# Re and im interleaved over partitions, half swaps with a stride of two and five swap buffers, in an adaLN + long convolution + MLP kernel whose order is laid out anew

## Chip, cores and metric

The kernel runs on one core of one Trainium2 chip. The metric is the device time of the program in microseconds (us), lower is better. The page of a profile has its own length, the span: the time from the first to the last instruction of one profiled execution.

## What is computed

One block of a conditioned network over x = A_q, with B = 1, S = 2048 positions, D = 640 channels and a hidden width F = 1728, in bf16:

```python
mod = (silu(c) @ w_mod).reshape(...)            # sa, ca, ga, sb, cb, gb
h = layernorm(x) * (1 + ca) + sa                # plays q
k_shift = sum_t k_pad[t:t+S] * shift_k[:, 3-t]  # causal, 4 taps
kv = k_shift * v
y = irfft(rfft(pad(kv, 4096)) * rfft(pad(ssm_k, 4096)))[:S] + kv * ssm_D
x = x + ga * (h * y)                            # part A
h = layernorm(x) * (1 + cb) + sb
u = gelu(layernorm(h) @ w1)
# four quarters of u, moved by +1, -1, +2, -2 positions -> hs
x1 = h + hs @ w2
x = x + gb * (x1 + gelu(layernorm(x1) @ w3) @ w4)   # part B
```

Part A is a convolution over the whole sequence, done with Fourier transforms of length 4096; part B is a two-stage MLP with a mixing of positions in its first stage.

## The kernel before

**Layout.** The positions stand on the 128 partitions in 16 tiles of 128, with 640 channels on the free axis; channels come in 5 blocks (ND). All SBUF regions are made once and reused many times: Ra (the filter, later x_all, that is x), Rb (inputs of the first stage, then products TAB, then y_all), T01 (its halves T0 and T1: data between the two transform stages, later weights w3 and w4), R3 (spectrum of kv, later the gelu results), R5 (k and v, then the spectrum of the filter, then h_all and scratch), RG (table Gs, then w1 and w2), RH (table Hs), RK, RQ. PSUM has four places.

**Stages.** Tables of sines come first: angles (L306 to L310), the Sin calls (`turns_to` L316, `sin_to` L321), the second-stage table Gs with its negated part (L348) and its copies to other partitions (L353, L354), the tables EA and EB of the inverse (L370). Then for both filter and kv: 32x32 transposes (`to_slots`, DVE, L394), first stage matmuls (L407) and second stage matmuls (`stage2_half`, L427), each followed by an evacuation of PSUM on ACT (L207) or DVE (L209). The result of a second stage has real parts on partitions 0 to 63 and imaginary parts on 64 to 127. The matmul of L463 makes k_shift. The modulation vectors are matmuls too (`mod_half`, L493, its weights loaded at L487). The layer norm of x (`ln1_stats`: DVE L539 and L540, or ACT L547 and L548; `ln1_fin` on POOL, L557 to L562) and the products that make q (`make_q`, L601 and L602, with the normalisation at L592 on ACT or L594 on DVE) are spread between these.

The complex product of the two spectra needs, beside a spectrum, the same spectrum with real and imaginary halves exchanged. `inverse1` does this ten times (5 blocks by 2 halves): two DMAs of 256 KB (L613, one issued by SP, one by POOL) exchange the halves into one of four buffers KSY, two DVE products follow (L617, the two in the tables TA and TB), then two groups of matmuls (L628 with EA, L629 with EB) and two evacuations. `inverse2` (matmul L661) makes y for up to three tiles in one PE task with two PSUM places. An identity matrix for PE's transposes is made on POOL (L644, shown as masks.py 197 and 199).

Part B runs over groups of tiles. `chain_a` multiplies y by q (L737), adds to x (L740) and squares on ACT (L729); `ln_finish` (POOL, L702 to L717) makes the statistics; `chain_b` applies the first norm (L751 or L756, and L755); `chain_c` the second (L724, or L592 and L594), and a `turn` transposes the tile by DMA (L765) or on PE (L772, evacuated at L778). `mm_w1` is L818 with gelu at L820, with an extra block of 32 rows (L828, gelu at L834); `mm_w2` L873 with its evacuation at L880; `mm_w3` L907 with gelu at L911; `mm_w4` L937 (and L928), the results added at L960 and L966 and stored at L969. Weights come by DMA: w1 and w2 at L992 to L995, w3 and w4 at L1009 to L1014. POOL fills up the last block of w3 (`L1020`). x is loaded in two parts (`x_load`, L525), the second with a dependence on the first tile of y (the list `y0`).

**What sets the order.** Every step is a task of a class Planner with the engine it may run on, its cost, and the regions it reads and writes. The order of all tasks, the engine of each and the PSUM place are not searched at run time, but written out in the string ORDER (L26 to L65); each word is a task's number, a letter for its engine (P, A, D, G for POOL, S for SP) and PSUM places. `Planner.run` (L120) emits the tasks in exactly this order:

```python
        for word in ORDER.split():
            head, _, places = word.partition(":")
            t = self.tasks[int(head[:-1])]
            t.on = self.CODE[head[-1]]
            assert t.deps <= seen and len(places) == len(t.alloc)
```

An engine runs its own tasks in that order and waits where data, a buffer or a PSUM place isn't there yet. In this order the 20 swaps run alternately on SP and POOL, of the 16 copies into Hs (L576) 7 are on SP and 9 on POOL, the identity comes after the last swap, and inverse2 of tiles 5 to 7 and 11 to 13 stand after the first w1 group.

Of the kernel before, what the change touches and what calls it, by code (L numbers as in the profile page):

```python
# [26 lines left out]
0S 2S 19G 18D 50G 20D 21G 23D 22D 25A 4S 3S 1S 6S 27G 29D 36G 37G 28D 5S 8S 9S 11S 68G 10S 69D 24A 26G 88P:0 72G 73D 31A 30A 32D 38G 66D 89A 84P:1 85A  # L27
67D 90P:2 91A 86P:3 87D 39G 40A 102P:0 103A 100P:1 76P:2 70G 104P:0 41D 49G 101A 77A 42G 43G 105A 106P:3 107A 44A 45G 33S 47S 46S 71D 34S 12S 35S 48S
184S 181S 183S 182S 13S 14S 116P:1 92P:2 98P:0 74D 75D 117D 7S 99A 118P:3 119D 114P:0 15S 112P:1 113D 93A 110P:2 16S 115A 111A 96P:3 97A 94P:0 95D
82P:2 83A 80P:1 81A 78P:3 108P:0 51D 109A 52D 54A 56G 57D 53A 122P:2 79D 155P:1 156A 153P:0 154A 151P:3 152A 123D 157P:2 136D 120P:1 121D 173P:0 158A  # L30
55G 174A 171P:3 172A 177P:2 178D 175P:1 176A 161P:0 162D 141P:3 142A 167P:2 168D 147P:1 148A 58G 59G 163P:0 164D 165P:3 166A 137P:2 138A 145P:1 146A
230D 17S 149P:0 150A 190D 188D 126P:3 127D 139P:2 140A 60A 143P:1 199S 144A 124P:0 125D 179P:2 180A 187D 169P:3 170A 234P:1 235A 244P:2 159P:0 160A
128P:3 231D 242P:1 243A 245A 130P:0 61G 62G 186D 63G 64A 238P:1 239A 129D 131D 232D 248P:2 65G 196S 249A 246P:3 247A 185D 189G 191A 252P:0 202S 253A
134P:1 135D 132P:2 133D 236P:3 240P:1 237A 260P:0 261A 233D 250P:2 251A 241D 423D 200P:3 201A 258P:0 259D 319G 208S 192G 268P:2 269A 318S 197P:3 205S
198A 266P:1 267A 272P:2 273D 270P:3 271A 203P:0 284P:1 285A 292P:2 211S 204D 278P:3 279A 417D 276P:0 277A 342S 293D 426D 209P:1 210D 294P:2 295D 226S
290P:3 222G 291A 280P:1 281D 229G 227S 264P:0 274P:2 275D 343G 223G 265A 256P:3 262P:1 420D 206P:0 207D 257A 225G 254P:2 255D 282P:3 263A 286P:0
288P:1 287D 224G 312P:2 220S 283A 289A 212P:3 321D 320D 218G 213D 313A 328D 304P:0 305A 308P:1 316P:2 317A 217S 216G 302P:0 219S 214G 418D 228S 298P:2
215S 324P:3 325D 309A 221G 327G 326S 329D 322P:1 303A 336D 306P:0 299A 421D 323A 310P:2 296P:3 307A 334S 335G 337D 350S 297A 311A 300P:1 330P:0 301A
351G 332P:3 344D 345D 331A 314P:2 333A 315A 359G 340P:1 341A 338P:0 352D 348P:3 349A 353D 346P:2 358S 347A 360D 361D 354P:1 367G 339A 356P:3 368D 366S
369D 355A 364P:2 357A 375G 362P:0 376D 372P:1 374S 377D 401S 193A 363A 382S 370P:3 373A 384D 383G 385D 380P:0 378P:1 365A 392D 390S 391G 393D 422D  # L40
419D 424D 402P:2 427D 194D 403D 371A 388P:3 381A 379A 407S 389A 428D 386P:0 387A 416G 425D 396P:1 397A 394P:3 395A 398S 399P:0 400D 432P:12 429A 430D
434D 433A 489D 502A 510D 195G 413S 490D 491A 511D 530D 408P:3 513D 404S 405P:0 406A 531D 409A 512A 440S 492G 494D 475P:12 476A 477A 515D 532A 462P:03
463A 410S 411P:1 493G 495D 514G 435S 533D 534G 496A 497D 498G 441G 535D 464A 516D 536D 518D 499D 412A 517A 469P:20 537A 471A 519G 500P:3 538D 539G
414P:1 465G 470A 558D 449S 501D 520D 521P:3 436S 415A 507P:0 522A 443S 559D 560A 540D 541P:2 437S 542A 466P:13 431D 561D 562D 563A 564D 508A 546P:2
467D 468A 547A 548P:1 565G 448S 570D 528P:0 571D 566D 572D 567D 549A 573A 446S 568D 505P:3 506A 569A 574G 575G 447S 509G 529A 503D 523D 504D 621D 622D
472P:21 473A 526P:3 527A 623A 579D 580P:0 581A 576D 439S 543A 524D 577P:2 525D 624D 578D 625D 444S 438S 550P:3 627D 480S 551D 481S 626A 590P:0 591A
445S 482S 552A 588P:2 589A 595P:3 459D 628G 633D 629D 634D 553G 630D 631D 632A 635D 637D 636A 479S 554G 555D 556P:0 557A 592P:2 486S 596D 597A 638G
641A 639D 478S 488G 610P:3 612P:0 611A 593D 608P:2 606P:3 544D 594A 598D 613A 599G 474D 460A 603D 600D 601P:1 604P:0 609A 457D 607A 442S 454A 602A
640S 642S 651P:2 649P:3 461G 650A 450D 487S 652A 485S 605D 673P:0 667P:1 451D 545D 668A 674A 452G 582D 583D 484S 689D 690D 456A 458G 584D 585D 656P:3
692D 693D 653P:2 483S 614P:1 654D 655A 657D 694A 615D 659G 658A 671P:0 695D 660G 664D 665P:2 691A 661D 662P:3 663D 453D 669P:1 696G 701A 702D 703D  # L50
666A 735P:3 455G 672A 670A 697D 698D 699D 705G 737P:2 736A 739P:0 733P:1 616D 704A 643D 644D 645D 700A 738A 706G 709A 675P:32 710S 586D 587D 740A 755D
756D 757A 646A 707D 708S 758D 759D 717P:0 714D 761G 760A 762G 734A 763A 767D 777A 768D 711A 769D 719P:1 764D 780D 676P 718A 720A 721P:0 724P:1 647D
712D 765D 766A 677D 678D 770A 680S 771G 772G 683D 741P:32 648D 773D 774S 722D 775A 776S 785P:0 725D 726A 783P:1 713D 723A 824D 617S 825D 742P 821D
822D 827D 679S 681S 826A 743D 682S 727G 728G 731D 732S 823A 784A 828G 829A 786A 787P:3 729D 730S 833D 834D 835D 830D 831D 832A 837D 684D 685S 836A
620S 838G 790P:1 788D 789A 839D 840S 799P:0 791D 805P:3 806A 781D 841D 715D 716D 881D 749D 793G 792A 882D 842S 883A 803P:1 804A 794G 795A 796S 845P:2
846A 797D 778D 779D 884D 843P:3 844A 885D 887D 800A 801P:1 802A 618S 847P:2 848D 782D 941D 850P:3 851D 852A 886A 849A 619S 687S 798S 865P:0 866A
859P:1 860A 863P:2 807P:30 861P:1 744D 750D 753S 942D 944D 745S 853D 854G 855A 888G 893A 943A 752S 857A 889D 864A 945G 890D 856S 808P 858S 809D 891D
946A 947D 948D 950D 894D 862A 892A 895D 896A 897G 925P:2 926A 898G 751S 815D 747S 919P:3 901D 686S 920A 923P:1 899D 921P:0 949A 951G 922A 902S 900S
905P:2 906A 688S 903P:3 904A 952D 953S 956P:0 957A 954P:2 955A 907P:3 908D 910P:0 810D 958G 748S 959P:2 911D 913G 746S 816D 819S 924A 962P:1 867P:30
960D 817S 963D 813S 754S 912A 993P:2 909A 914G 812S 868P 915D 916S 917D 918S 977P:1 978A 994D 995A 996G 997G 971P:2 820S 972A 869D 998A 875D 927P:30  # L60
818S 964A 814S 811S 876D 961A 965D 966G 973P:1 967A 999S 969A 970S 870D 929D 974A 1028P:2 930D 975P:3 928P 968S 1000P:1 1001A 931S 935D 1002P:0 934S
976A 979P:13 981D 1003A 1006P:0 871S 873S 1004P:1 879S 1005A 872S 874S 936D 980P 987D 1029A 937S 933S 1026P:1 939S 1007A 877S 932S 988D 1024P:2 1025A
1032D 880S 878S 982D 983S 1008P:30 986S 991S 1027A 989S 1033D 1010D 938S 940S 1022P:2 1011D 1023A 1014S 1013S 1009P 1016D 984S 985S 1017D 1030P:13
1034D 992S 990S 1015S 1012S 1018S 1019S 1020S 1035D 1037S 1036S 1021S 1038S 1031P 1040D 1039S 1041D 1043A 1045A 1042S 1044S
# [72 lines left out]
def kernel(  # L137
# [45 lines left out]
    Gs = RG[:, 0:6144].rearrange("p (k n) -> p k n", k=32)  # L183
# [8 lines left out]
    KSY = [(RG[:, 6144:8192], ("RG", 6144, 8192)), (RK[:, 0:2048], ("RK", 0, 2048)), (RK[:, 2048:4096], ("RK", 2048, 4096)), (Rb[:, 8192:10240], ("Rb", 8192, 10240))]  # L192
# [55 lines left out]
    offc = mem.tile([P, 6], F32, name="offc")  # L248

# [64 lines left out]
    def turns_to(dst, xs, n, r, w, neg=False):  # L314
        sc = (-2.0 if neg else 2.0) * PI_LO
        add("ACT", 0.23 + 0.00083 * n, lambda e: nc.scalar.activation(dst, xs, ACT.Sin, scale=sc), r=[r], w=[w])  # L316

    def sin_to(dst, ms, q, n, r, w, neg=False):
        b = (b_neg if neg else b_pos)[dst.start_partition():dst.start_partition() + dst.shape[0], :]
        sc = (2.0 if neg else -2.0) * PI_LO / q  # L320
        add("ACT", 0.25 + 0.00095 * n, lambda e: nc.scalar.activation(dst, ms, ACT.Sin, scale=sc, bias=b),  # L321
            r=[r, ("consts", 0, 1)], w=[w])
# [12 lines left out]
    for kb in range(2):  # L335
        o = (5120, 6656)[kb]
        k2s = slice(8 * kb, 8 * kb + 8)
        wk = ("RG", 1536 * kb, 1536 * kb + 1536, "g")
        pat, base = [[2, 8], [128, 64]], 1 + 16 * kb
        if kb == 0:  # L340
            ms, ma, ky = angles("R3", o, 512, pat, base, s64[:], 8192, (offc[:, 0:1], offc[:, 1:2]))
            ms3, ma3 = (t.rearrange("p (a b) -> p a b", a=8) for t in (ms, ma))
            sin_to(Gs[:, k2s, 64:128], ma3, 8192, 512, ky[1], wk)
            sin_to(Gs[:, k2s, 0:64], ms3, 8192, 512, ky[0], wk)
        else:
            for i, (xs, xk) in enumerate(angles_pool("R3", o, 512, pat, base, s64t[:], (offc[:, 2:3], offc[:, 3:4]))):
                turns_to(Gs[:, k2s, 64 * i:64 * i + 64], xs.rearrange("p (a b) -> p a b", a=8), 512, xk, wk)
# [300 lines left out]

    def inverse2(tilesA):
        n = len(tilesA)  # L650
        pss = [Slot() for _ in range(2)]

        def f(e):
            for s in pss:
# [424 lines left out]
```

## Time and profile before

| what | value |
|---|---|
| device time, three runs | 302.31, 302.04, 301.63 us; median 302.04 |
| span of the profiled execution | 298.7 us |
| what lies around the span, against the median | 3.3 us |
| PE busy | 269.7 us, 90% |
| DVE busy | 218.2 us, 73% |
| ACT busy | 208.3 us, 70% |
| POOL busy | 104.8 us, 35% |
| DMA traffic | 35.76 MB, 120 GB/s as a mean |

The page's share of a chain is the part of the span for which that engine's work was what the last-ending chain consisted of:

```profile
PE 51%; DVE 13%; ACT 11%; DMA 10%; POOL 6%; issue 5%; SPq 2%; DVEq 0%; POOLq 0%; ACTq 0%
```

Busy time is no measure of a limit by itself, since the stages have different ones: the first 110 us are made of many elementwise steps on DVE and ACT, the last 160 of large matmuls. A slice of the page is 7.5 us long.

### The profile page before, as it was taken

The numbers are of one execution on the slowest core, as the hardware profiler recorded it, in microseconds if no ns is written. First come the engines' busy times: TensorE is split into PE (matmuls) and PEld (weight loads), VectorE is DVE, ScalarE is ACT, GpSimd is POOL, SyncE is SP. The second block draws the span as 40 slices with busy tenths as digits, with TensorE's granted clock in tenths as the row PEclk, the third lists the DMA queues.
The fourth block names the chain that finished last, engine by engine and source line by source line (L and its number), as shares of the span: only waits on it lengthen the run. The fifth ranks groups of instructions, "written<-read, shape, count | busy, mean of one in ns | idle before, by whom it ended". The sixth has DMA issues, their size and how long they took to land.

```text
span 298.7 us, 7890 instructions
## 1 busy us (share of the span) xinstructions
PE 269.7 (90%) x3176; PEld 208.5 (70%) x3182; DVE 218.2 (73%) x438; ACT 208.3 (70%) x341; POOL 104.8 (35%) x237
## 2 busy tenths in 40 slices
PE   0999999999989766869999999999999999999993
PEld 0666755777878436648878677787788767887871
DVE  8998999999999998898759589886361544212442
ACT  4799989999999789979868775766854705431200
POOL 5864364453216591434275426120421321100000
PEclk9999999999999859799999999999999999999999
DMA  6999999898999920563700203223113030510112
GB/s 215 275 215 184 225 137 246 225 217 221 229 253 281 280 65 2 153 203 69 273 4 0 46 5 68 56 46 60 41 40 80 5 89 6 63 43 23 29 52 60
DMA packets 58356, 35.76 MB, mean 120 GB/s; under 512 B 40032, under 2 KB 55008, under 8 KB 58320
## 3 DMA queue, kind: packets, MB, share of 16 engines
q1 hardware_dynamic: 57136, 32.01, 46.3%
q0 software_dynamic: 1088, 3.21, 4.1%
q8 instruction: 25, 0.41, 0.6%
q14 instruction: 11, 0.09, 0.1%
q10 hardware_dynamic: 96, 0.04, 0.1%
HBM read 16.31 MB, written 2.62 MB: 63 GB/s over the span
## 4 chain that ended last, share of the span: by engine, by line
PE 51%; DVE 13%; ACT 11%; DMA 10%; POOL 6%; issue 5%; SPq 2%; DVEq 0%; POOLq 0%; ACTq 0%
PE ps_w L937 17%; PE ps_w L907 14%; ACT T L207 5%; DMA Ra<-in_A_q_dram 5%; PE ps_w L873 4%; PE ps_w L818 3%; PE ps_s L427 3%; ACT RG L729 3%; DVE Rb L617 3%; PE ps_ksh L463 2%; POOL lnv L715 2%; PE ps_s L407 2%; DMA RK<-R 2%; DVE R L756 2%; PE ps_mod L493 2%
## 5 line engine op out<-in xcount | busy, mean ns | idle before, releaser
L907 PE MATMUL ps_w<-R,T 128*128 128x256 bf16 (+1 forms) x630 | 63.8, 261 | 0.7 <-DMA R<-RH 0.7
L907 PEld LDWEIGHTS <-T 128*128 128x128 bf16 x630 | 55.5, 98 | 7.9 <-issue 2.0
L937 PE MATMUL ps_w<-T,R 128*128 128x320 bf16 x416 | 59.1, 299 | 0.0
L911 ACT ACTIVATE R<-ps_w 128x1024 bf16<-128x1024 f32 (+2 forms) x36 | 28.8, 827 | 41.9 <-PE ps_w L907 41.9
L937 PEld LDWEIGHTS <-R 128*128 128x128 bf16 x416 | 40.5, 98 | 15.2
L960 DVE TENSOR_TENSOR T<-ps_w,R 128x640 bf16<-128x640 f32 x15 | 12.3, 822 | 35.4 <-PE ps_w L928 18.1
L207 ACT CAST T<-ps_s 128x1024 bf16<-128x1024 f32 x32 | 30.4, 1029 | 3.2 <-PE ps_s L407 3.1
L207 ACT CAST R<-ps_s 128x960 bf16<-128x960 f32 (+1 forms) x35 | 30.8, 964 | 1.8 <-PE ps_s L427 1.6
L407 PE MATMUL ps_s<-F1bd,Rb 128*128 128x256 bf16 x160 | 23.3, 298 | 8.7 <-DVE Rb L394 8.1
L729 ACT ACTIVATE RG<-R 128x640 bf16<-128x640 bf16 x32 | 23.5, 734 | 9.9 <-DVE R L880 6.7
L407 PEld LDWEIGHTS <-Rb 128*128 128x128 bf16 x160 | 16.7, 107 | 14.7 <-DVE Rb L394 8.6
L873 PE MATMUL ps_w<-RG,R 128*128 128x320 bf16 x160 | 23.2, 299 | 2.1 <-ACT R L820 2.1
L715 POOL TENSOR_TENSOR lnv<-lnv,mhalf 128x2 f32<-128x2 f32 (+1 forms) x29 | 22.5, 775 | 2.3
L427 PE MATMUL ps_s<-T,RG 64*128 64x160 bf16 x512 | 21.2, 230 | 0.8 <-ACT R L207 0.6
L880 DVE SCALAR_TENSOR_TENSOR R<-ps_w,R 128x640 bf16<-128x640 f32 x16 | 12.9, 819 | 11.8 <-PE ps_w L873 11.6
L427 PEld LDWEIGHTS <-RG 64*128 64x128 bf16 x512 | 17.7, 94 | 5.1 <-issue 4.6
L818 PE MATMUL ps_w<-R,RG 128*128 128x256 bf16 (+1 forms) x200 | 20.0, 259 | 1.3 <-DMA R<-RK 0.6
L873 PEld LDWEIGHTS <-R 128*128 128x128 bf16 x160 | 15.4, 98 | 8.2 <-ACT R L820 2.4
L629 PE MATMUL ps_i<-EB,Rb 128*128 128x128 bf16 x160 | 19.0, 219 | 1.5 <-DVE Rb L617 1.4
L818 PEld LDWEIGHTS <-RG 128*128 128x128 bf16 x200 | 17.1, 102 | 3.5 <-issue 2.0
L628 PE MATMUL ps_i<-EA,Rb 128*128 128x128 bf16 x160 | 19.0, 219 | 0.4 <-ACT R L207 0.3
L714 POOL TENSOR_TENSOR lnv<-stat,lnv 128x2 f32<-128x2 f32 x19 | 4.0, 212 | 40.9 <-ACT RG L729 28.7
(178 smaller groups left out, 513.5 us busy)
## 6 DMA issues: line engine op xcount, KB each, us to landing
Ra<-in_A_ssm_k_dram SPq DMA_DIRECT2D x5, 512.0 KB, 5.7
R<-in_w_mod_dram SPq DMA_DIRECT2D x6, 400.0 KB, 6.0
out_dram<-RH SPq DMA_DIRECT2D x60, 40.0 KB, 1.6
T<-in_B_w_dram SPq DMA_DIRECT2D x5, 432.0 KB, 6.2
RH<-in_w_mod_dram SPq DMA_DIRECT2D x4, 400.0 KB, 4.4
Ra<-in_A_q_dram SPq DMA_DIRECT2D x4, 320.0 KB, 6.6
RK<-R SPq DMA_DIRECT2D x5, 256.0 KB, 4.5
RK<-R POOLq DMA_DIRECT2D x5, 256.0 KB, 5.3
```

Source lines behind the costliest of these rows:

```text
L207: nc.scalar.copy(dst, src(ps.tile))
L407: nc.tensor.matmul(psv[:, ml, :], lhsT=xL[:, s0:s0 + P], rhs=F1r, start=True, stop=True)
L427: nc.tensor.matmul(psv[:, g, j], lhsT=Gs[p, k, 64 - 64 * cc:192 - 64 * cc], rhs=T1h[h][p, cc * 32 + k], start=(cc == 0), stop=(cc == 1), t ...
L628: nc.tensor.matmul(psv[:, w, :], lhsT=Av[:, r_, :, g_], rhs=EAf, start=True, stop=False)
L629: nc.tensor.matmul(psv[:, w, :], lhsT=Bv[:, r_, :, g_], rhs=EBf, start=False, stop=True)
L715: nc.gpsimd.tensor_tensor(rs, rs, mhalf[:, 0:n], ALU.pow)
L729: add("ACT", 0.74, lambda e: nc.scalar.activation(junk, src, ACT.Square, scale=float(D) ** -0.5, accum_out=stat[:, li, 1, t:t + 1]), r=[sk ...
L818: nc.tensor.matmul(pt[:, fb, 0:cw], lhsT=w1_sb[:, b, 160 * fb:160 * fb + P], rhs=hT[:, b, 0:cw], start=(b == 0), stop=(b == ND - 1))
L873: nc.tensor.matmul(pt[:, hf, 0:320], lhsT=gsf[:, fb, c0:c0 + P], rhs=w2_sb[:, fb, 320 * hf:320 * hf + 320], start=(fb == 0), stop=(fb == 4))
L907: nc.tensor.matmul(pt[:, fl, 0:cw], lhsT=w3_sb[:, b, fb * P:(fb + 1) * P], rhs=xT[:, b, 0:cw], start=(b == 0), stop=(b == ND - 1))
L911: nc.scalar.activation(g3[g % 2][:, f0:f0 + fn, 0:cw], ps.tile[:, 0:fn, 0:cw], ACT.Gelu_apprx_tanh)
L937: nc.tensor.matmul(bank(i, hf), lhsT=gg[:, fb, i * P:(i + 1) * P], rhs=w4_sb[:, fb, 320 * hf:320 * hf + 320], start=(fb == 0 and i == 0), ...
```

## The change

- The output columns of Gs are laid out anew, so that real and imaginary parts of a frequency stand on neighbouring partitions. Gs grows from 192 to 256 columns per index and takes all of RG; two negating operations per block take the place of one; its copies move 262 KB instead of 196.
- EA and EB follow: frequency and sign per partition come from two new columns (`half_p`, `sgn_p`), and each table is written in one operation over 128 partitions instead of two over 64.
- The exchange of halves reads every second partition and writes every second partition.
- There are five swap buffers instead of four: two of them lie in Ra, none in RG any more.
- The later modulation weights, w3, g3 and the scratch tiles `ut` have other places: w3 goes from T0 to R5, g3 from R5 to T0, `ut` to free parts of R3 and R5.
- Loads of w1, w2 and the second part of x no longer depend on y. In the new order all x loads and all Hs copies are issued by SP; POOL keeps its half of the swaps.
- A call of gelu on one column is added on ACT, behind the first evacuation of inverse2.
- Inverse2 is split in two PE tasks with one PSUM place each.
- ORDER is written anew: among other things all of inverse2 now comes before the first w1 group, chain_a of group 3 comes before chain_c of group 0, the identity comes between swaps, w1 of groups 7, 8 and 9 come earlier and w4 later. Numbers of tasks change, their number per engine hardly.

```diff
-    Gs = RG[:, 0:6144].rearrange("p (k n) -> p k n", k=32)
+    Gs = RG[:].rearrange("p (k n) -> p k n", k=32)
+    Gv = RG[:].rearrange("p (k c j t) -> p k c j t", k=32, c=2, t=2)
...
-    KSY = [(RG[:, 6144:8192], ("RG", 6144, 8192)), (RK[:, 0:2048], ("RK", 0, 2048)), (RK[:, 2048:4096], ("RK", 2048, 4096)), (Rb[:, 8192:10240], ("Rb", 8192, 10240))]
+    KSY = [(Ra[:, 5120:7168], ("Ra", 5120, 7168)), (Ra[:, 7168:9216], ("Ra", 7168, 9216)), (RK[:, 0:2048], ("RK", 0, 2048)), (RK[:, 2048:4096], ("RK", 2048, 4096)), (Rb[:, 8192:10240], ("Rb", 8192, 10240))]
...
+    half_p, sgn_p = lnv[:, 0, 0:1], lnv[:, 0, 1:2]
...
-            sin_to(Gs[:, k2s, 64:128], ma3, 8192, 512, ky[1], wk)
-            sin_to(Gs[:, k2s, 0:64], ms3, 8192, 512, ky[0], wk)
+            sin_to(Gv[:, k2s, 1, :, 1], ma3, 8192, 512, ky[1], wk)
+            sin_to(Gv[:, k2s, 1, :, 0], ms3, 8192, 512, ky[0], wk)
...
-        add(("POOL", "DVE"), {"POOL": 1.48, "DVE": 0.35}, lambda e, k2s=k2s: eng_of[e].tensor_scalar(Gs[:, k2s, 128:192], Gs[:, k2s, 0:64], -1.0, None, ALU.mult),
+        for i in range(2):
+            add(("POOL", "DVE"), {"POOL": 1.49, "DVE": 0.62}, lambda e, k2s=k2s, i=i: eng_of[e].tensor_scalar(Gv[:, k2s, 0, :, i], Gv[:, k2s, 1, :, 1 - i], 1.0 - 2.0 * i, None, ALU.mult),
...
+        eng.tensor_single_scalar(pci[:, 0:1], pidx[:], 1, ALU.arith_shift_right)
+        eng.tensor_single_scalar(pci[:, 1:2], pidx[:], 1, ALU.bitwise_and)
+        eng.tensor_copy(half_p[:], pci[:, 0:1])
+        eng.tensor_scalar(sgn_p[:], pci[:, 1:2], -4.0 / LFFT, 2.0 / LFFT, ALU.mult, ALU.add)
...
-            for o in range(2):
-                eng_of[e].tensor_scalar(E[64 * o:64 * o + 64, i, :], src[64 * o:64 * o + 64, :], sg[o], None, ALU.mult)
+            eng_of[e].tensor_scalar(E[:, i, :], src, sg, None, ALU.mult)
...
-                                nc.tensor.matmul(psv[:, g, j], lhsT=Gs[p, k, 64 - 64 * cc:192 - 64 * cc], rhs=T1h[h][p, cc * 32 + k],
+                                nc.tensor.matmul(psv[:, g, j], lhsT=Gs[p, k, 128 * cc:128 * cc + 128], rhs=T1h[h][p, cc * 32 + k],
...
-        ky, kk = KSY[i % 4]
+        ky, kk = KSY[i % 5]
...
-            dma("SP" if o == 0 else "POOL", 256, lambda q, o=o: q.dma_start(ky[64 * o:64 * o + 64, :], kx[64 - 64 * o:128 - 64 * o, :]), r=[kxk], w=[kk + ("y",)], rate=222.0)
+            dma("SP" if o == 0 else "POOL", 256, lambda q, o=o: q.dma_start(ky[o::2, :], kx[1 - o::2, :]), r=[kxk], w=[kk + ("y",)], rate=390.0)
...
-        pss = [Slot() for _ in range(2)]
...
         for i in range(2):
-            t2 = evac(yv[:, 2 * i:2 * i + 2], lambda t: t[:, :, 0:160 * n].rearrange("p j (a u) -> p j a u", a=n), 320 * n, pss[i],
+            ps = Slot()
...
-    w3_sb = T0[:, 0:ND * FP].rearrange("p (b n) -> p b n", b=ND)
+    w3_sb = R5[:, 10240:10240 + ND * FP].rearrange("p (b n) -> p b n", b=ND)
...
-    g3 = [R5[:, 10240 + 3584 * i:10240 + 3584 * (i + 1)].rearrange("p (f n) -> p f n", f=NF) for i in range(2)]
+    g3 = [T0[:, 3584 * i:3584 * (i + 1)].rearrange("p (f n) -> p f n", f=NF) for i in range(2)]
...
+    add("ACT", 0.25, lambda e: nc.scalar.activation(s64[:], b_pos[:], ACT.Gelu_apprx_tanh),
+        r=[("consts", 0, 1), ("sin", 0, 1)], w=[("gelu", 0, 1), ("scol", 0, 1)])
...
-    x_load(8, 12, y0)
-    x_load(12, NT, y0)
+    x_load(8, 12)
+    x_load(12, NT)
```

## The prediction, made before the changed kernel ran

> **What bounds the kernel now.** I read the page's slices first, then windows of ten microseconds, then the chain of waits, then single lines. The slices say that the limit changes on the way:
>
> ```profile
> PE   0999999999989766869999999999999999999993
> DVE  8998999999999998898759589886361544212442
> ACT  4799989999999789979868775766854705431200
> ```
>
> Each digit is 7.5 us. DVE and ACT are full from 10 us to about 110, PE is full from about 140. The windows (PE, PEld, DVE, ACT, POOL, then the granted clock, the DMA share and GB/s) put numbers on the change of regime:
>
> ```profile
> 80.00:90.00 10.00, 8.60 (x142) 7.86 (x142) 10.00 (x10) 9.97 (x14) 1.53 (x3) 1.00 1.01 248
> 100.00:110.00 10.00, 5.76 (x201) 3.06 (x201) 9.74 (x28) 9.18 (x21) 8.17 (x12) 0.64 0.72 166
> 120.00:130.00 10.00, 8.95 (x167) 6.91 (x164) 8.51 (x25) 9.40 (x24) 4.71 (x16) 0.84 0.69 219
> 140.00:150.00 10.00, 9.69 (x88) 8.21 (x89) 8.30 (x23) 8.60 (x20) 3.59 (x10) 1.00 0.68 223
> ```
>
> At 80 to 90 us, in the middle of the inverse transform, DVE has no gap and the DMA engines none either. At 100 to 110 PE does least, at a clock of 0.64. From 140 PE holds. The turning point is the first w3 matmul, and these lines lie around it:
>
> ```profile
> 92.57 1.22 DVE L617 TENSOR_TENSOR Rb<-R,RK 128x2048 bf16<-128x2048 bf16 x1
> 115.56 1.28 ACT L834 ACT_TABLE_LOAD   x1
> 135.49 0.45 POOL L1020 COPY T<-T 128x320 bf16<-128x320 bf16 x1
> 135.74 0.67 PE L907 MATMUL ps_w<-R,T 128*128 128x128 bf16 x9
> ```
>
> The last product of the spectra ends at 93.7; 42.2 us later, at 135.94, w3 begins, straight behind the end of POOL's copy (the row's 135.74 is the start of a group of nine whose length is modelled). From there to the last matmul (294.0) are 158 us. Summing issue intervals (56 ns at 128 columns, 109 at 256, 136 at 320), I get 155 us of matmul work in them and 2 to 2.5 us of stall, of which two pieces of the chain are the cause:
>
> ```profile
> 167.93 2.65 DMA R<-RK
> 203.88 2.58 DMA R<-RH
> ```
>
> There a DMA transpose holds up w1 of group 5 (PE stalls 1.13 us) and w3 (0.82 us). So the end is the time of the first w3, plus 155 us, plus the stalls, plus a tail of 4.7 us. A change gains only if it brings the first w3 forward or removes stalls behind it.
>
> **What the Trainium skill says.** "SBUF — State Buffer", "Door 1: The DMA port swizzle": a transfer over partitions 0 to 63 reaches half of the 16 ports, one over all 128 all of them, with 196 against 328 GB/s measured there. The old swap reads one half and writes the other. The new one has on each side every second partition, so all ports: an estimate of 256 KB / 328 GB/s = 0.8 us instead of 1.3 each if alone. The trace shows 3.1/5.2/7.3 us to landing (min/median/max) among other traffic, so no run here shows the bare rate. "DMA: Bandwidth & Descriptors", "Issuing engines are not separate DMA queues": moving loads to SP saves issue time only. Issues take 0.46 to 0.58 us on SP and 0.51 on POOL here. "ScalarE: Activation LUTs", "What ACT_TABLE_LOAD costs": 1283 ns; the trace agrees with 1.28.
>
> **Part by part.** *Until the last product.* Swaps and fifth buffer: 20 products of 1.135 us (start to start) run on DVE from 68.44 on, and 70 to 90 us shows DVE 9.87 and 10.00. The view of the swaps' line lists who ended the waiting of the queues that issue them:
>
> ```profile
>   DVE Rb L617: 7.7, 4
> ```
>
> The swaps wait for products to free a buffer (7.7 us), and the products' own view names no product that waited for a swap. A faster swap or a fifth buffer removes nothing from a full DVE: worth 0. If the cover goes, third swap first: its SP half stands behind 16 Hs copies (16 x 0.58 = 9.3 us of SP; before, 7 were on SP, 9 on POOL); bounds 0 and +1, I take +0.2. The identity (0.20 + 3.69 us of POOL) now stands between swaps; the buffers run two swaps ahead: 0.
>
> Added work: the interleaved table needs two half negates per block, three of four on DVE, against one on DVE and one on POOL: +2 x 0.74 = +1.5 on DVE. Two sign and half columns: four 1-column operations, +0.6 by the nearest row (L444 on one column, 0.15 each). Matmuls of stage 2 keep 128 contiguous columns; sin writes with step two, which no row shows: bounds 0 and, were the rate halved, +0.64 for each of four (L316's 0.64, all ACT), I take 0, since ACT has gaps before 15 us. E tables fall from 8 x 0.365 to 4 operations on POOL, which has slack. Work that the new order shifts before the last product: stage 2 evacuations on DVE 8 instead of 5 (+3 x 1.15) and q products (+1.4), less two statistics (-2.2), one evacuation and one normalisation (-1.65) and two angle operations (-1.1): in all DVE +2.1, ACT +1.4 (two statistics of 1.64 in, evacuations out). DVE was idle for 2.8 us between 1 and 100, so of the +2.1 between -1 and +2 shows: I take +0.5 in all with the swaps.
>
> *From the last product to the first w3.* By rows, in the new order: group 0's affine (L724) comes at +20.7 instead of +15.5, since the second inverse2 and group 3's chain_a now stand ahead of it; but what they displace is done, and w2 of tile 1 is evacuated at +32.4 instead of +34.3. Three things help. The table load leaves the chain: it now sits behind the first inverse2 evacuation, where ACT has 0.34 + 1.11 us of gaps: -1.28, of which up to 0.3 comes back there. Inverse2 split in two tasks starts its evacuation half a block earlier. w3 no longer waits for Zh's space: the transpose's evacuation ended at 135.28, and the copy held w3 until 135.94: -0.66. First w3 at about +40.0: -2.2. Its bounds are -4 and -0.5, since I placed some 60 tasks by hand. x loads without their wait on y start earlier; in the chain they carry 8.41 and 5.34 us, but what follows them there (POOL L715) had come due 0.5 us before anyway, and the tiles they bring are needed 30 us later: 0.
>
> So the first w3 comes +0.5 - 2.2 = -1.7 relative to before.
>
> *After it.* PE's work is the same, only stalls can differ. I counted for each matmul group PE's work since the first w3, less the work that DVE and ACT must do before it since w2 of tile 1. A smaller number is a tighter place:
> - w3 of group 2: DVE -3.5 (before -0.7)
> - w1 of group 5: DVE +4.9, ACT -1.8 (before +2.4, +5.7)
> - w1 of groups 6 to 8: between -2.1 and +2.0 (before +6.5 to +23)
> - from w3 of group 4: over +5.
>
> w1 of groups 7 to 9 has been brought forward, so the elementwise chain of those tiles is due earlier. Engines have a head start here (7.6 us on DVE, 4 to 5 on ACT), which covers every negative number, the worst by some 2.7, about one DMA transpose. Stalls: bounds 0.5 and 6 us, where before has 2 to 2.5. I take 2.7: +0.4.
>
> Sum against the profiled execution: 298.7 - 1.7 + 0.4 = 297.4 of span, and the 3.3 us by which the median exceeds that span stay: 300.7.
>
> **Rivals.**
> *Gain given back (slower).* Mechanism: ACT and DVE fall behind at w1 of groups 5 to 8, where PE stood 0.5 to 1.1 us per place before. For: ACT was 8.6 of 10 busy at 140 to 150, and the margin there falls by 4 to 20 us. Against: from 210 us ACT and DVE have large gaps, and PE can run w4 while it waits. Price: three places at 1.2 to 2.5 us, stalls of 5.5 to 7, that is +3.3 to +4.7 over before's, less 1.7: 303.6 to 305. It decides once the extra stalls exceed 1.7 us.
> *Nothing gained.* Of the added DVE work 1.6 us shows instead of 0.5, and the hand placement is 0.2 too good: +1.6 - 2.0 + 0.4 = 0, so 302.0. For: DVE at 10.00. Against: two named waits go in any case.
> *Larger gain.* The new order also fills DVE's 2.8 us of idle time before 100 us, and stalls stay as they are: 300.7 - 2.8 - 0.4 = 297.5. For: the DMA engines at 1.01 share in 80 to 100, which faster swaps relieve, so that Hs copies and x come in time. Against: added work of 2.1.
>
> **Numbers.** Small gain as summed, 298.6 to 301.4: 0.43. Larger gain, below 298.6: 0.14. No change that a measurement can tell (within 0.2%, 301.4 to 302.6): 0.12. Slower: 0.31. So faster 0.57. The range 296.8 to 304.8 leaves out some 0.1 at each end; the likeliest case alone has 298.6 to 301.4.
>
> **What would show it.** Right: the products at 1.135 us without gaps; no table load between inverse2 and w1; L907's first group at 133 to 135; stalls behind it of 2 to 3.5 us. Wrong: gaps before the third or fourth product (swap late behind the Hs copies); a last product beyond 95.5; PE idle over 4 us in 150 to 210 with ACT at 9.5 or more there (the slower rival); a first w3 before 132 (the larger gain).

## The result, and the profile after

The changed kernel takes 312.13 us (median of 312.91, 312.62, 311.65 and 311.01), the kernel before beside it 302.18: 1.0325 times as long, with a 95% interval of 1.0288 to 1.0362. The forecast was 300.7 within 296.8 to 304.8: a gain of 1.5 us was expected, and a loss of 9.95 came. The profiled execution of the changed kernel has a span of 311.2 us against 298.7. The times of the versions below are medians of all executions, while their ratios leave out those over 1.5% above a version's fastest. The kernel before was timed beside every set of versions (medians of 301.66 to 302.80), so versions of different sets are best compared by their ratios.

Four marks in the two traces, all of them starts, divide these 12.5 us. The product of spectra is L628 in the changed kernel (L617 before), the first w3 matmul L920 (L907 before). The 12.5 are more than the 9.95 of the medians for a reason: other executions on record last 1.7 to 2.2 us longer than their span, so the profiled one of the kernel before lies about 1.5 us under its median (an estimate: 302.04 - 1.8 - 298.7), and that of the changed kernel, at 312.91, is the longest of its four.

| stretch | before | after | difference |
|---|---|---|---|
| start to first product | 68.44 | 73.76 | +5.3 |
| first to last product | 24.13 | 33.94 | +9.8 |
| last product to first w3 | 43.17 | 40.74 | -2.4 |
| first w3 to the end | 162.96 | 162.76 | -0.2 |

The last two rows are what the prediction built its number on, and they came out nearly as it said. The loss is in the first two, for which it had taken +0.5 together. The first row depends on the execution: seven traces of kernels that share the order up to the first product, the copies into Hs apart, have that product at 72.19 to 74.26 us, 3.8 to 5.8 later than before.

The slices of the changed kernel (7.8 us each) show the hole at once: the twelfth and thirteenth digits, 9 for DVE and ACT before, are 7 and 2 for DVE and 3 and 2 for ACT, and PE falls to 2 in the twelfth.

```profile
PE   0779999999727987488999999999899999999994
DVE  8999979999672999988899899994034422400423
ACT  4789999899932999989999989997637122042020
```

The windows of the same kernel (PE, PEld, DVE, ACT, POOL busy, then granted clock, DMA share, GB/s), and under them the one of the kernel before from 90 to 100:

```profile
80.00:90.00 10.00, 5.93 (x102) 5.01 (x99) 7.17 (x7) 7.75 (x9) 2.68 (x5) 1.00 0.95 320
90.00:100.00 10.00, 4.46 (x37) 4.09 (x38) 2.21 (x3) 1.01 (x1) 0.71 (x1) 0.66 0.90 288
95.50:99.00 3.50, 3.46 (x33) 3.49 (x34) 0.00 (x0) 1.01 (x1) 0.71 (x1) 0.50 1.01 337
```

```profile
90.00:100.00 10.00, 9.30 (x230) 7.63 (x227) 9.86 (x19) 8.63 (x10) 5.88 (x8) 1.00 1.02 293
```

Before, DVE was busy for 10.00 and 9.86 us of the two windows from 80 to 100; now for 7.17 and 2.21. In the second of them none of the computing engines is even half busy: they wait. The DMA engines aren't idle, at 0.90 here and 1.02 before. DVE's own timeline (start, duration, what; in brackets the idle time before and who ended it) shows three stops among the products:

```profile
80.98 1.23 DVE L628 TENSOR_TENSOR Rb<-R,RK 128x2048 bf16<-128x2048 bf16 x1 [1.06 <-DMA RK<-R]
...
85.59 1.22 DVE L628 TENSOR_TENSOR Rb<-R,RK 128x2048 bf16<-128x2048 bf16 x1 [1.85 <-DMA RK<-R]
...
99.15 1.23 DVE L628 TENSOR_TENSOR Rb<-R,Ra 128x2048 bf16<-128x2048 bf16 x1 [7.79 <-PE ps_i L640]
```

The first two stops wait for a swap (into RK), the third for PE. A product of block 6 writes the table that block 4's matmuls read, so DVE must wait until PE is through with block 4. And PE waits too, for a DMA, as its timeline and the view of its line L639 (who ended its idle time: us, times) say:

```profile
95.54 0.27 PE L639 MATMUL ps_i<-EA,Rb 128*128 128x128 bf16 x1 [6.76 <-DMA Rb<-R]
```

```profile
  issue: 6.9, 1
  DMA Rb<-R: 6.8, 1
  DVE Rb L628: 1.8, 3
```

The DMA named is the last swap, of block 9, into columns 8192 to 10240 of Rb. The matmuls of block 4 read tables in columns 0 to 4096. They share no byte. (The view counts matmuls and weight loads apart; the 6.9 us are the weight load's share of the same wait.) In the kernel before, the same line (L628 there) names one wait for ACT and no DMA:

```profile
  ACT R L207: 0.3, 1
```

The issues on SP (start, duration of all, what) say why the third swap is late, and when the last one is issued:

```profile
66.05 12.37 SPq L587 DMA_DIRECT2D RH<-RK  x16
78.52 0.54 SPq L624 DMA_DIRECT2D RK<-R  x1
...
90.39 0.61 SPq L624 DMA_DIRECT2D Rb<-R  x1
```

SP's half of the third swap stands behind all sixteen copies into Hs, which take 12.37 us of the queue; the swap of block 9 is issued by POOL at 89.08 and by SP at 90.39, and lands at 92.87 and 95.41. PE starts at 95.54. From 88.8 to 95.5 us the DMA engines are busy for 0.98 of the time, with w1 and modulation weights too, so the time that this swap takes, and with it PE's wait, may owe something to these loads; no run took them away alone.

The late start has a different look: no hole, but more busy time. Until the first product DVE is busy for 69.25 us instead of 64.86 (+4.4) and idle for 0.9 more, which is the whole of the 5.3. ACT has 63.15 instead of 58.80. Where operations overlap, each counts from the end of the one ahead. Of DVE's +4.4, evacuations of PSUM are then +2.9 (20 instead of 17), twelve operations on angles +2.0 (L296 and L297, L292 and L293 before, with the same count), the products for q +0.9, negations of Gs +0.8, statistics -1.6; smaller items make up the rest. The first stage begins 1.3 us late already: its first evacuation on ACT starts at 10.46 instead of 9.19.

Later DVE waits once for x, of which the statistics need the first tiles: the load is now issued at 30.68 behind copies of Gs, before at 26.45.

```profile
41.90 0.89 DVE L550 BATCH_NORM_STATS2 ln_st<-Ra 128x6 f32<-128x320 bf16 x2 [1.61 <-DMA Ra<-in_A_q_dram]
```

After the products all goes well. PE's timeline around the turning point:

```profile
148.44 0.72 PE L920 MATMUL ps_w<-R,R 128*128 128x128 bf16 x10
```

### The profile page after: what moved, and what is told of

It reads as the page before. It is cut to its first block, busy times and chain, and to the rows that moved or that the text cites. A ratio compares the mean times of both kernels' runs of the same rounds, so it can differ in the third digit from the quotient of the medians.

```text
span 311.2 us, 7927 instructions
## 1 busy us (share of the span) xinstructions
PE 271.0 (87%) x3182; PEld 211.1 (68%) x3182; DVE 217.0 (70%) x431; ACT 216.6 (70%) x357; POOL 104.7 (34%) x234
## 4 chain that ended last, share of the span: by engine, by line
PE 51%; DVE 15%; ACT 13%; DMA 10%; issue 5%; SPq 3%; DVEq 0%; ACTq 0%
PE ps_w L950 15%; PE ps_w L920 13%; PE ps_w L886 5%; PE ps_w L831 4%; ACT RG L740 4%; DVE Rb L406 3%; PE ps_mod L505 3%; DMA Ra<-in_A_q_dram 3%; DVE Rb L628 2%; DMA RK<-R 2%; DMA R<-RK 2%; DMA RG<-RG 2%; PE ps_s L439 2%; PE ps_s L419 2%; DVE R L480 2%
## 5 line engine op out<-in xcount | busy, mean ns | idle before, releaser
L920 PE MATMUL ps_w<-R,R 128*128 128x256 bf16 (+1 forms) x630 | 64.1, 261 | 0.1
L924 ACT ACTIVATE T<-ps_w 128x1024 bf16<-128x1024 f32 (+2 forms) x36 | 29.1, 826 | 47.2 <-PE ps_w L920 35.4
L920 PEld LDWEIGHTS <-R 128*128 128x128 bf16 x630 | 55.6, 98 | 6.7 <-issue 0.7
L950 PE MATMUL ps_w<-T 128*128 128x320 bf16 x416 | 59.2, 299 | 0.0
L950 PEld LDWEIGHTS <-T 128*128 128x128 bf16 x416 | 40.2, 98 | 16.2 <-issue 1.1
L209 ACT CAST R<-ps_s 128x960 bf16<-128x960 f32 (+1 forms) x32 | 28.8, 969 | 1.5 <-PE ps_s L439 1.5
L419 PEld LDWEIGHTS <-Rb 128*128 128x128 bf16 x160 | 16.8, 105 | 17.1 <-DVE Rb L406 9.4
L639 PE MATMUL ps_i<-EA,Rb 128*128 128x128 bf16 x160 | 20.9, 229 | 7.8 <-DMA Rb<-R 6.8
L209 ACT CAST T<-ps_i 128x1024 bf16<-128x1024 f32 x20 | 19.4, 1052 | 9.5 <-PE ps_i L640 9.3
L640 PE MATMUL ps_i<-EB,Rb 128*128 128x128 bf16 x160 | 20.5, 229 | 2.9 <-DVE Rb L628 2.8
L639 PEld LDWEIGHTS <-Rb 128*128 128x128 bf16 x160 | 16.4, 103 | 8.6 <-issue 6.9
L886 PEld LDWEIGHTS <-R 128*128 128x128 bf16 x160 | 15.4, 98 | 7.5 <-ACT R L833 1.7
```

The source lines that it names most:

```text
L209: nc.scalar.copy(dst, src(ps.tile))
L419: nc.tensor.matmul(psv[:, ml, :], lhsT=xL[:, s0:s0 + P], rhs=F1r, start=True, stop=True)
L639: nc.tensor.matmul(psv[:, w, :], lhsT=Av[:, r_, :, g_], rhs=EAf, start=True, stop=False)
L640: nc.tensor.matmul(psv[:, w, :], lhsT=Bv[:, r_, :, g_], rhs=EBf, start=False, stop=True)
L886: nc.tensor.matmul(pt[:, hf, 0:320], lhsT=gsf[:, fb, c0:c0 + P], rhs=w2_sb[:, fb, 320 * hf:320 * hf + 320], start=(fb == 0), stop=(fb == 4))
L920: nc.tensor.matmul(pt[:, fl, 0:cw], lhsT=w3_sb[:, b, fb * P:(fb + 1) * P], rhs=xT[:, b, 0:cw], start=(b == 0), stop=(b == ND - 1))
```

## The experiments

Three theories stood behind the runs, under these letters. **A**: the stride of two in the swap makes PE's matmuls on the tables wait for the swap into Rb, though neither touches the other's columns. **B**: the swaps come late because SP issues them behind sixteen copies into Hs. **C**: the new order and the added work start the products late, or other changes cost the time, and the swaps are only where it shows. Each could be most of the loss by the profile alone.

### The stride by itself: `halves` and `before_stride`

Two edits of one line in opposite directions: `halves` is the changed kernel with the swap of before, `before_stride` the kernel before with the swap of the change. In both, the rows that are exchanged don't fit the layout of the table, so other rows are multiplied with each other; bytes and instructions are the same, and so is each engine's order.

```diff
 halves, against the changed kernel (L624)
-q.dma_start(ky[o::2, :], kx[1 - o::2, :])
+q.dma_start(ky[64 * o:64 * o + 64, :], kx[64 - 64 * o:128 - 64 * o, :])
 before_stride, against the kernel before (L613)
-q.dma_start(ky[64 * o:64 * o + 64, :], kx[64 - 64 * o:128 - 64 * o, :])
+q.dma_start(ky[o::2, :], kx[1 - o::2, :])
```

> The changed kernel, but the swap moves whole halves of 64 partitions again, while tables and spectra stay interleaved: the products then multiply other rows, so the numbers of the convolution change and the work does not. Theory A (the transform's matmuls wait for a swap that lies in Rb beside their tables, because of its stride of two): the weight loads' waits for swap transfers go, DVE's hole of 7.8 us before 99 us goes, time 304 to 306. Theory B (the swaps stand behind 16 Hs copies on SP): unchanged holes of 1.1 and 1.9 us, time 311 to 313. Theory C (the order as such starts the products late and spreads them): 311 to 313.

> The kernel before with the changed kernel's swap pattern alone: every second partition is read and written, four buffers, old order. The halves of a spectrum are then not the ones that are exchanged, so the numbers of the convolution change and the work does not. Theory A: the stride alone brings the wait; the matmuls behind block 7's swap into Rb stand until it has landed (before, these swaps took 5 us), so 3 to 6 us on top: ratio 1.01 to 1.02. Rival (the wait needs the new order or the fifth buffer): ratio 0.995 to 1.005. Rival (16 ports pay): below 0.995.

`halves` took 306.02 us (one run; span 304.3), 6.1 less than the changed kernel. PE's line L639 has no DMA left among those that end its idle time; its longest entry (matmuls and weight loads together) is

```profile
  DVE Rb L628: 2.7, 5
```

Holes of 2.92 and 1.77 us before the third and fourth product remain, and 1.56 later.

`before_stride` took 308.32 us, 1.0203 times the kernel before [1.0160, 1.0246]. The view of its matmul line and two lines of PE's timeline:

```profile
  DMA Rb<-R: 10.4, 4
```

```profile
88.88 0.23 PE L628 MATMUL ps_i<-EA,Rb 128*128 128x128 bf16 x1 [2.56 <-DMA Rb<-R]
```

```profile
93.90 0.29 PE L628 MATMUL ps_i<-EA,Rb 128*128 128x128 bf16 x1 [2.42 <-DMA Rb<-R]
```

Nothing but the partitions of one DMA was changed here: no new order, no fifth buffer, no added work. PE goes from no wait on that transfer to two, of 4.98 us together; the view has each of them twice, for the matmul and for its weight load. The wait also runs the other way. SP's half of block 7's swap waits for PE's matmuls before it is issued, and a product then waits for that swap. The issue in the kernel before; then what SP waited for, the issue and the product in `before_stride`:

```profile
80.19 0.46 SPq L613 DMA_DIRECT2D Rb<-R  x1
```

```profile
SPq L613 <- PE ps_i L629: 10.7, 1, 10.7
```

```profile
91.50 0.46 SPq L613 DMA_DIRECT2D Rb<-R  x1
```

```profile
93.97 1.23 DVE L617 TENSOR_TENSOR Rb<-R,Rb 128x2048 bf16<-128x2048 bf16 x1 [2.82 <-DMA Rb<-R]
```

The products take 30.26 us from first to last instead of 24.13, and the first w3 goes from 135.74 to 142.54. (In the changed kernel the same wait of the swap for PE is small: POOL waits 1.43 us before it issues block 9's swap.) A is shown, at some 6 us in either kernel. The transfer itself became quicker: 2.2/3.6/5.9 us to landing (min/median/max) instead of 3.1/5.2/7.3. That agrees in direction with what the Trainium skill says in "SBUF — State Buffer", "Door 1: The DMA port swizzle", on which the prediction drew. It gained nothing, since no product had waited for it.

### The swap of block 9 elsewhere, the copies on two queues: `i9_ra`, `hs_split`, `i9_ra_hs`

`i9_ra` puts block 9's swap into the first buffer in Ra, so that no strided write goes into Rb so late, and behind block 5's products in ORDER, since Ra must be free; three x loads move behind it. `hs_split` leaves the buffers alone and hands eight of the sixteen Hs copies to POOL. `i9_ra_hs` is both.

```diff
 i9_ra
-        ky, kk = KSY[i % 5]
+        ky, kk = KSY[0 if i == 9 else i % 5]
 hs_split, in ORDER
-229S 228S 218S 221S 227S 219S 220S 217S
+229G 228G 218G 221G 227G 219G 220G 217G
```

> The changed kernel with the last swap (i = 9) in Ra, the place that block 5 has left, instead of Rb, issued behind block 5's products; three x loads go behind the last product. The output is the same. Theory A: the weight load's late wait for a transfer goes and with it the 7.8 us hole on DVE; 304 to 306. Theory B: 310 to 313, the hole only moves to another swap. Theory C: 311 to 313.

> The changed kernel with every second of the 16 Hs copies on POOL. Theory A: the first two holes (1.1 and 1.9 us) shrink, the large one stays; 309 to 312. Theory B: SP comes to the third swap 5 to 6 us earlier, all later swaps too, and the large hole goes as well; 303 to 306. Theory C: 311 to 313.

> Both edits together: last swap in Ra, Hs copies on two queues. Theory A with B as a smaller part: 301.5 to 303.5, no hole over 1 us among the products. Theory B alone: as hs_split. Theory C: 311 to 313.

`i9_ra` took 306.53 us, 1.0153 times before [1.0084, 1.0223]. The hole of 7.79 is gone, but block 9's swap is now itself late, as DVE's timeline has it (its trace is of the longest of four executions, 309.68 us):

```profile
100.05 1.23 DVE L628 TENSOR_TENSOR Rb<-R,Ra 128x2048 bf16<-128x2048 bf16 x1 [2.99 <-DMA Ra<-R]
```

`hs_split` took 309.87 us (one run). SP gets to the third swap seven microseconds sooner (1.6 of them because the copies begin sooner in this trace), and the products of blocks 2 and 3, from 77 to 82 us, follow without a gap; then A's hole stands where it stood:

```profile
64.47 6.94 SPq L587 DMA_DIRECT2D RH<-RK  x8
71.51 0.54 SPq L624 DMA_DIRECT2D RK<-R  x1
```

```profile
94.76 1.23 DVE L628 TENSOR_TENSOR Rb<-R,Ra 128x2048 bf16<-128x2048 bf16 x1 [8.04 <-PE ps_i L640]
```

So A and B are two separate waits, the first worth 5.6 or 6.1 us of the time (`i9_ra`; `halves`, one run), the second 2.3 (`hs_split`, one run), against 2.91 of hole in the trace. By the ratios to the kernel before, which was 0.6 us slower beside these versions, these come to 5.2, 6.6 and 2.8 us. `i9_ra_hs` took 304.02 us (20 runs), 1.0028 times before [1.0000, 1.0055]. Together the two account for 8 to 9 of the 10 us. That no hole over 1 us would stay in `i9_ra_hs` did not come true: 3.30 us before a product of block 9 are left in its trace, that of its longest execution.

### What is left: `i9_free`, `i9_free_again`, `i9_free_x`

In `i9_ra_hs` SP's half of block 9's swap still stood behind a w1 load and modulation weights. `i9_free` issues both halves on POOL and moves the w1 load behind two x loads. `i9_free_again` is the same kernel, timed more often. `i9_free_x` also puts the first four x loads ahead of the last two Gs copies on SP, to take away the wait for x.

```diff
 i9_free, against i9_ra_hs
-            dma("SP" if o == 0 else "POOL", 256, ...
+            dma("SP" if o == 0 and i < 9 else "POOL", 256, ...
 i9_free_x, in ORDER: 186S 184S 187S 185S moved behind 34S
```

> The changed kernel with the last swap in Ra, both its halves issued by POOL, Hs copies on two queues, and the load of w1 behind two loads of x, so that this swap shares the DMA engines with less. Same output. If what is left among the products is the late landing of that swap (3.3 us in the run with both edits): hole under 1.5 us, and the mod's hole of 2.6 us goes, first w3 at 138 to 140, span 2 to 4 us under that run's 305.6. If the DMA engines are full whatever the order: hole over 2.5 us.

> The changed kernel with the last swap in Ra and on POOL, Hs copies on two queues, w1 behind two x loads, timed in rounds now. If the wait in Rb and the full SP queue are the whole loss of the change, its predicted gain must come out: ratio 0.990 to 0.997. If the later start of the products (4.1 us in its profile) takes the gain: ratio 0.998 to 1.006.

> As i9_free, and the first four loads of x stand on SP ahead of the last two copies of the Gs table. Theory: the 1.6 us hole on DVE at 39 us goes, products start 1 to 1.6 us earlier, and the time falls by as much against i9_free: 299 to 301, below the kernel before (ratio 0.985 to 0.997). Rival: the table copies come late instead and stage 2 waits: no gain against i9_free.

`i9_free` took 302.84 us once and, as `i9_free_again`, 302.39 (20 runs), 1.0012 times before [0.9990, 1.0034]. PE's timeline of `i9_free` at its first w3:

```profile
138.86 0.55 PE L920 MATMUL ps_w<-R,R 128*128 128x128 bf16 x7
```

Its products run from 72.56 to 96.76, 24.20 us, as before (24.13). So the whole of the second row of the table was swap waits. What it has in addition to the kernel before is the start, 4.1 us late, and what it gains is 1.1 us up to the first w3 and 0.8 after it. The trace of `i9_free_again` says the same of the last two (1.1 and 0.9), but has its start 5.8 us late: one and the same kernel differs by 1.7 us there from one execution to another.

`i9_free_x` was a miss: 308.87 us, 1.0218 times before [1.0182, 1.0254]. The wait for x is gone, but the x loads and a transpose whose issue takes 6.34 us now stand ahead of the Gs copies, and the second stage waits for the table. SP and DVE:

```profile
34.61 1.18 SPq L359 DMA_DIRECT2D RG<-RG  x2
```

```profile
40.34 1.16 DVE L211 CAST R<-ps_s 128x960 bf16<-128x960 f32 x1 [4.92 <-PE ps_s L439]
```

A hole of 1.6 us was bought off with one of 4.9. In this place the x loads cost more than they save. That another place can't take the late start back isn't shown.

### The table load: `no_preload` and `before_preload`

`no_preload` makes the added call on ACT an Identity, so that gelu's table is loaded where gelu is first used (its base is `i9_free_x`). `before_preload` adds the call of gelu to the kernel before, behind the first evacuation of inverse2.

```diff
 no_preload
-nc.scalar.activation(s64[:], b_pos[:], ACT.Gelu_apprx_tanh)
+nc.scalar.activation(s64[:], b_pos[:], ACT.Identity)
 before_preload
+    add("ACT", 0.25, lambda e: nc.scalar.activation(s64[:], b_pos[:], ACT.Gelu_apprx_tanh), w=[("gelu", 0, 1)])
```

> i9_free_x with the added column operation as identity instead of gelu (nothing uses its result), so that the gelu table is loaded in front of the first w1 gelu again. If the table load on the chain is worth its 1.28 us: first w3 0.8 to 1.3 us later than in i9_free_x. If it is covered there: under 0.3 us.

> The kernel before with one more column operation: gelu on one column on ACT behind the first evacuation of inverse2, nothing else. If the table load of 1.28 us was on the chain to the first w3: first w3 0.8 to 1.3 us earlier, ratio 0.995 to 0.998. If the chain had slack there: 0.999 to 1.001.

`no_preload` took 310.84 us (one run); from last product to first w3 42.51 us instead of 41.55 in its base, so the early load is worth about 1.0 there, though a larger hole ahead (6.35 instead of 4.92) blurs this. `before_preload` took 302.61 us, 1.0020 times before [0.9999, 1.0041], and the stretch to w3 43.05 instead of 43.17. ACT's timeline shows that the load does leave its old place, and where the gain goes:

```profile
99.85 1.28 ACT L1045 ACT_TABLE_LOAD   x1
...
116.22 1.09 ACT L834 ACTIVATE R<-ps_w1x 32x128 bf16<-32x128 f32 x4
...
125.83 0.69 ACT L778 COPY R<-ps_tr 128x640 bf16<-128x640 bf16 x1 [0.58 <-PE ps_tr L772]
...
128.12 0.74 ACT L729 ACTIVATE RG<-Ra 128x640 bf16<-128x640 bf16 x1 [0.78 <-DVE Ra L740]
```

Counted from the start of the last product, the first gelu of w1 comes at 22.90 us instead of 24.28. But then ACT waits for PE and DVE, 1.70 us in three places up to 129.3 where the kernel before has one wait of 0.42, and a later gelu of w1 (L834) comes at 35.98 instead of 35.78. The time freed on ACT is lost to waits for other engines ahead of w3.

### A better version: `best2` and `best3`

`best2` is `i9_free` with the last negation of Gs on DVE placed ahead of the inverse tables' angles. `best3` also restores the old place of the first-stage table, ahead of the others.

```diff
 best2, in ORDER: 47D moved behind 46D
 best3, in ORDER: 23D behind 22D, 24A behind 25A, 26G 39G 40G behind 71G, 41A behind 90A, 42G behind 41A
```

> As i9_free, and the last negate of the Gs table on DVE stands before the angles of the inverse tables instead of behind them, so that the copies of Gs and the first x loads behind them on SP start about 1.7 us earlier. If the late table sets the late start: the 1.6 us hole before the first statistics goes, products start at 70.5 to 71.5 instead of 72.6, 1 to 2 us less than i9_free. If only the added DVE work does: start within 0.5 us of i9_free.

> As best2, and the first stage's small table (the angles of F1, their sine and its spread on POOL) stands ahead of the angles of Gs again, as in the kernel before, with one scaling of angles on POOL instead of DVE. Theory: the first transpose starts at 6.0 us instead of 7.3 and the first evacuation 1.2 us earlier, the products start 0.8 to 1.3 us earlier than in best2: ratio 0.992 to 0.996. Rival: the Gs table comes later by this and keeps the start where it is: ratio 0.996 to 1.000.

`best2` took 301.60 us, 0.9978 times before [0.9954, 1.0002], `best3` 302.22, 1.0018 [0.9991, 1.0044]. `best2` starts its products at 72.01, 0.55 us sooner than `i9_free`, nearly what its second theory said, and 1.1 us of the 1.6 us wait for x stay. `best3` brought the first evacuation on ACT back to 9.09, but its products begin at 72.75. By these traces the first 1.3 us of lateness don't carry through. Both differences are smaller than the 1.7 us between two executions of one kernel. So this, and that the late start is mostly the sum of added DVE work further on, is only argued. Against the changed kernel `best2` wins by about 10 us. Against the kernel before it can't be told from no change.

## Why the prediction was wrong, step by step

**The step that failed** is "Swaps and fifth buffer: [...] worth 0", with its "bounds 0 and +1, I take +0.2" if the cover goes. The finding in it was right: no product had waited for a swap, so a faster one gains nothing. It asked only what the swap's quickness removes, not who would have to wait for the transfer in its new form. The new form adds a wait: the weight load of block 4's matmuls waits for both halves of block 9's swap. The half swaps in turn wait for PE's matmuls of block 3. Both waits are put in when the program is built, and are there in the list of semaphore waits of the built program; the prediction read the order of instructions, but not their waits. The bound of +1 left it out. It cost 6.76 us on PE, then about 1.6 more because PE resumed at half clock (32 matmuls of block 4 at 106 instead of 56 ns), of which DVE shows 7.79.

**The SP queue** was named, with its place ("third swap first: its SP half stands behind 16 Hs copies"), and mis-sized. The sixteen issues took 12.37 us rather than 9.3 (its 0.46 to 0.58 us for an issue on SP were too narrow for the old kernel too, whose swaps took up to 0.78), and two products waited, not one: 1.06 + 1.85 = 2.9 us, where +0.2 was taken. For the value of +0.2 between its bounds the prediction gives no reason; its remark that the buffers run two swaps ahead, made of the identity, is no help here either: both halves must have landed, and a queue runs in order.

**The added work** was mis-sized twice. In amount: until the last product's end DVE is busy for 93.20 us instead of 90.07, +3.1 where the sum had +2.1; ACT 86.79 instead of 84.08, +2.7 where it had +1.4. The sum had -1.1 for two angle operations (L306, 0.57 and 0.54 us) that leave DVE; one of 0.42 us is still there, so -0.7. What it left out are the other twelve: 3.97 us before, 6.02 after. Two of them make up the difference, on only 32 and 64 columns. Each took 1.2 us beside a POOL operation. DVE, then POOL:

```profile
6.17 1.20 DVE L297 TENSOR_SCALAR R<-R 128x32 int32<-128x32 int32 x1
...
20.26 1.24 DVE L296 TENSOR_SCALAR R<-R,lnv 128x64 int32<-128x64 int32 x1
```

```profile
6.06 1.26 POOL L314 TENSOR_TENSOR R<-R 128x512 f32<-128x512 f32 x1
...
20.13 1.32 POOL L314 TENSOR_TENSOR RK<-RK 128x512 f32<-128x512 f32 x1
```

The second of the two is in this trace alone; the versions' traces have that operation at 0.23 to 0.63 us.

And in how much of it shows: the sum let gaps absorb most ("I take +0.5"). On an engine with under 3 us of gaps in 100, nothing was absorbed, and 0.9 us of idle time came on top.

**The sin writes** with step two were costed at 0. They run 0.13 to 0.23 us longer each (644 to between 773 and 871 ns, 715 to 871 ns): above 0, far from the bound of 0.64.

**Last product to first w3**: predicted -2.2, measured -2.4. The total is right, its terms less so. The table load of -1.28 is worth 0.1 in the old order and about 1.0 in the new. In the versions built on `i9_ra` the stretch shrinks by only 1.1 (`i9_free`), 1.4 (`best2`) or 2.0 us (`best3`). The large hole, in which other engines might have caught up, isn't the likelier reason: `halves` doesn't have it and shrinks by 2.2, while in `i9_ra` it grows by 0.95. What sets these versions apart here is above all that three x loads stand behind the last product. No run moved those loads alone, so this stays argued.

**After the first w3**: predicted +0.4, measured -0.2. The slower rival, stalls of w1 groups 5 to 8, didn't come: between 150 and 210 us ACT is 96% busy, as it foresaw, yet PE is idle for only 0.44 us of the 60, where the rival's sign was over 4. The result is on that rival's side, but by none of its mechanism. Of the marks set out ahead, both under "Wrong" that concern the swaps came true: gaps before the third and fourth product, and a last product beyond 95.5 (107.70).

The sum put right, from the four marks: 298.7 + 5.3 + 9.8 - 2.4 - 0.2 = 311.2. Had the two waits been known and nothing else, the prediction's own 300.7 + 6 + 2.7 would have come to 309.4 (2.7 is the 2.9 less the 0.2 that it had taken).

Open: why the builder adds the wait for this pair (a write to every second partition, a weight read with a step in the free axis, in one region) and not for DVE's contiguous reads beside the strided swaps in Ra, how much shorter PE's wait would be with fewer loads on the DMA engines, and which of the added DVE operations before the first product could be hidden again. No run tried a fifth buffer outside Rb and Ra.

## What to carry to other kernels

When a transfer or an operand changes its shape, ask not only how long it takes but which instructions will now be taken to overlap with it; read the list of waits of the built program against the old one ahead of any duration, above all where two tenants share a region. A small transfer that something waits for must not be put behind a row of bulk copies on a queue that runs in order; count the issue time ahead of it. And relief on an engine whose work nobody waits for is worth nothing, while work added to a full engine showed in full here, +4.4 us of it in a start 5.3 us later.

## What the runs showed of the hardware

After 6.76 us without matmuls PE resumed with 106 ns from start to start instead of 56, at a granted clock of 0.50. The Trainium skill has these two figures in "TensorE: Matmul & The Clock Gate", "Part 1: The HAM clock gate" (106.7 and 55.6 ns at 128 columns, the slow one after an idle window of some 3.4 us); the trace agrees with both. It means that a wait of this kind costs more than its own length. The length of 3.4 us is no safe limit, though: the clock also fell to 0.50 after waits of 2.56 us in `before_stride` and 2.65 us in `halves`, each time within 1.2 us of PE's first matmul behind the wait, and stayed at 1.00 after one of 2.02 us in the changed kernel.

The operation of 1.20 us on 32 columns started 0.11 us after POOL's and ended with it, to within 0.05 us. In nine traces of the new order it is so, with 1.19 to 1.20 us. In `hs_split`, with the same order, POOL's operation starts later, behind this one, which then takes 0.18 us:

```profile
6.12 0.18 DVE L297 TENSOR_SCALAR R<-R 128x32 int32<-128x32 int32 x1
```

```profile
6.36 1.27 POOL L314 TENSOR_TENSOR R<-R 128x512 f32<-128x512 f32 x1
```

"SBUF — State Buffer", "Who interferes with whom" says that DVE in a mode that uses two ports, which `tensor_scalar` can enter, shares a port pair with GpSimd, and that whoever issues first blocks the other fully. These traces agree; which mode the operation ran in, none of them shows.

A 256 KB swap over every second partition landed in 3.6 us at the median instead of 5.2, in an otherwise equal kernel (`before_stride` and the kernel before), and in 4.8 instead of 6.4 in the other pair (the changed kernel and `halves`).
